# Moving the cosine and spectrum tiles of a three-stage spectral MLP kernel to other start addresses in SBUF

## Chip, cores and metric

One NeuronCore of a Trainium2 chip runs the whole program in one launch. The metric is the device time of that launch in microseconds (us); less is better. The engines are named as in the profile: PE is TensorE's matmuls, PEld its weight loads, DVE is VectorE, ACT ScalarE, POOL GpSimd, and SP the engine that issues most of the DMAs.

## What is computed

The input x has 4 batches of 3136 rows by 256 columns. Three layers follow each other, all in float32:

```python
def _attn_ref(x, filt_r, filt_i):                 # layer 0: a filter along the rows
    X = np.fft.rfft(x, axis=1)
    return np.fft.irfft(X * (filt_r + 1j * filt_i)[None], n=x.shape[1], axis=1)

def _moe_ref(x, w_ch1, w_ch2):                    # layer 1: two-dimensional FFT, then an MLP
    u = x + np.real(np.fft.fft(np.fft.fft(x, axis=1), axis=2))
    un = (u - mean(u)) / np.sqrt(var(u) + 1e-06)
    return u + np.maximum(un @ w_ch1, 0.0) @ w_ch2   # 256 -> 1024 -> 256

def _moe2_ref(x, g_ln, w_ch1, w_ch2):             # layer 2: a second MLP
    xn = (x - mean(x)) / np.sqrt(var(x) + 1e-06) * g_ln
    return x + np.maximum(xn @ w_ch1, 0.0) @ w_ch2
```

## The kernel before

**Spectrum.** The Fourier transforms of 3136 = 64 x 49 points are matrix products with small matrices of sines and cosines. Batch 0 goes first and alone (`first_p` and `first_q`, matmuls on L365, L382, L320, L426 and L454); batches 1 to 3 are done later, in pieces between the work of the MLPs (`over_p` and `over_q`, with the four-quadrant matmuls of `quarter` on L267 and the transposes on L618). Their results are a table `zt` of the filtered spectrum, in SBUF, and the half-transformed rows `vd`, in DRAM.

**Units.** The 12544 rows are handled as 24 units U of 512 rows and a last one of 256. `prep_ticks(U)` makes the input u of layer 1 for a unit: ACT and DVE split a slice of `zt` into a high and a low part (`zs`, tiles `zsh` and `zsl`, for the last unit `zslh` and `zsll`, with the copy `zmid` for one column), and PE multiplies these with a split cosine table (`chi`, `clo`) in 12 matmuls of 128 x 256:

```python
        for a in range(2):
            for eo in (1, 0):
                for i, (s, r) in enumerate(PASSES):      # ("h","h"), ("l","h"), ("h","l")
                    lhs = zmid[...] if eo == 0 and i == 2 else z[a][eo][s]
                    nc.tensor.matmul(out=ps[a][:, eo], lhsT=lhs, rhs=cs[eo][r], ...)     # L731
```

The operand `lhsT` is what PE holds still (a weight load, PEld, brings it), and `rhs` is what it streams past. So `zs` and `zmid` are loaded and `chi` and `clo` stream. Sixteen quarter matmuls of the rows `vr` (L267, 64 x 64 x 256) follow and end the unit's u.

**MLPs.** For each unit and layer the rows are normalised, turned (by transposes on PE, L831, or by a DVE transpose and a trip through DRAM) and split into `xth` and `xtl`. Then `w1_step` streams them against loaded weights `w1a` or `w1b` (L904), ACT and DVE evict the hidden rows into `hh` and `hl`, and `w2_step` loads these and streams `w2a` or `w2b` (L931). All operands of L731, L904 and L931 are 4-byte fp32r; each matmul has its own weight load, and each streams 256 columns.

**Order.** The order on every engine is written out by hand: eight hidden blocks of (U, layer) in turn, with the ticks of `prep_ticks`, `ln_ticks`, `over_p` and `over_q` hung on numbered steps. `prep_ticks` always puts its 12 matmuls behind a `w1_step` of the MLP and before the 16 quarter matmuls.

**Addresses.** SBUF tiles are laid out pool after pool, in the order in which the pools are opened. `gap(name, words)` opens a pool that holds one unused tile of so many 4-byte words, which pushes everything behind it. `PAD` is the list of the gaps' sizes.

Of the kernel before, what the change touches and what calls it, by code (L numbers as in the profile page):

```python
# [158 lines left out]
    return c.astype(np.float32)  # L159


PAD = (24, 16, 48, 48, 16, 32, 16)
NA, LAG = 3, 3
AHEAD = 3
DURING = {4: 'a', 8: 'a', 12: 'a', 16: 'a', 18: 'k', 20: 'a', 24: 'ac', 26: 'a', 28: 's', 30: 'f', 31: 'c', 33: 'f', 34: 'c', 35: 'f', 37: 'f', 38: 'c'}
# [18 lines left out]
def spectral_mlp_kernel(ctx: ExitStack, tc, x, ff, ff0, cst, w1a, w2a, gln, w1b, w2b, out):  # L184
# [4 lines left out]
    def pool(name, bufs, **kw):  # L189
        return ctx.enter_context(tc.tile_pool(name=name, bufs=bufs, **kw))  # L190

    def gap(name, words):
        pool(name, 1).tile([128, words], F32, name=name)

    sm = pool("sm", 4)
    head = pool("head", 1)
    gap("gap0", PAD[0])
    keep = pool("keep", 1)
    gap("gap1", PAD[1])
    keep64 = pool("keep64", 1)  # L200
    uop = pool("uop", 1)
    gap("gap2", PAD[2])
    wp1 = pool("wp1", 1)
    gap("gap3", PAD[3])
    wp2 = pool("wp2", 1)
    wps = {"1": wp1, "2": wp2}
    dram = pool("dram", B, space=DRAM)
    ztp = pool("ztp", 2)
    gap("gap4", PAD[4])
    zsp = pool("zsp", 1)  # L210
    raw = pool("raw", 2)
    vrp = pool("vrp", 2)
# [6 lines left out]
    up = pool("up", 3)  # L219
    xnp = pool("xnp", 1)  # L220
    xdp = pool("xdp", 2, space=DRAM)
    gap("gap5", PAD[5])
    xtp = pool("xtp", 2)
    gap("gap6", PAD[6])
    hp = pool("hp", 2)
    banks = pool("banks", 8, space=PSUM)

# [897 lines left out]
def _launch(inputs):  # L1125
# [58 lines left out]
    with tile.TileContext(nc) as tc:  # L1184
        spectral_mlp_kernel(tc, *args)
# [22 lines left out]
```

## Time and profile before

| | us |
|---|---|
| median of 3 runs | 1345.98 |
| lowest and highest of them | 1345.86, 1347.0 |
| the profiled execution, its own time | 1346.94 |
| its span, first to last instruction | 1345.2 |

PE is busy for 1317.5 us of the span, PEld for 1211.0, DVE for 796.5, ACT for 616.9, POOL for 270.5. Busy time of PE overlaps itself: one matmul takes some 280 ns from start to end, and the next one starts some 113 ns after it. So the pace of PE is read from the distance between starts, and a group of n matmuls in the timeline has n such distances up to the start of the next group. The granted clock of TensorE is at full speed for nearly the whole span (mean 0.992).

### The profile page before, as it was taken

The page shows a single profiled execution, that of the slowest core. Times are in us where ns is not written, and L with a number is a line of the kernel's source. Part 1 is how long each engine was busy: PE and PEld are TensorE (multiplying, and loading weights), DVE is VectorE, ACT ScalarE, POOL GpSimd, SP SyncE. Part 2 cuts the span into 40 slices and gives each one's busy share as a digit, 9 for nine tenths or more (in the row PEclk, how much of TensorE's full clock was granted, in tenths as well). Part 3 has the DMA queues.
Part 4 walks back from the last instruction along what each step waited for, and adds up shares of the span by engine and source line. Part 5 has one row for each costly group of instructions (what it writes and reads, how often), then busy time and mean ns, then how long its engine had stood idle before and what let it go on. Part 6 is the DMA issues. An engine that isn't in the chain of part 4 may idle for free.

```text
span 1345.2 us, 27766 instructions
## 1 busy us (share of the span) xinstructions
PE 1317.5 (98%) x11221; PEld 1211.0 (90%) x11221; DVE 796.5 (59%) x1643; ACT 616.9 (46%) x1205; POOL 270.5 (20%) x277
## 2 busy tenths in 40 slices
PE   8969999999999999999999999999999999999998
PEld 6527998899989989999988999999999999999998
DVE  5968875666454666656454665656555555465453
ACT  5646544454435444544434544545434443444322
POOL 1763012332040222212032221312000000000000
PEclk9979999999999999999999999999999999999999
DMA  8754323443544634623353535534221413332200
GB/s 315 253 192 146 101 92 76 154 115 86 134 140 136 153 91 116 165 62 95 89 170 104 161 106 123 147 81 111 56 64 48 95 34 77 80 83 45 64 17 24
DMA packets 214920, 147.97 MB, mean 110 GB/s; under 512 B 163516, under 2 KB 187196, under 8 KB 214792
## 3 DMA queue, kind: packets, MB, share of 16 engines
q1 hardware_dynamic: 198056, 117.36, 33.6%
q10 hardware_dynamic: 16736, 28.84, 5.9%
q8 instruction: 88, 1.44, 0.5%
q14 instruction: 40, 0.33, 0.1%
HBM read 87.71 MB, written 58.46 MB: 109 GB/s over the span
## 4 chain that ended last, share of the span: by engine, by line
PE 92%; DVE 4%; DMA 1%; ACT 1%; issue 1%; POOL 1%; SPq 0%; ACTq 0%; DVEq 0%; POOLq 0%
PE ps L931 39%; PE ps L904 38%; PE ps L267 7%; PE ps L731 2%; PE ps L320 2%; PE ps L365 1%; PE ps L426 1%; PE ps L618 1%; PE ps L831 1%; PE ps L382 0%; DVE hl L914 0%; DMA vd<-vst 0%; DVE bs L775 0%; DMA gd<-gst 0%; DVE wm L873 0%
## 5 line engine op out<-in xcount | busy, mean ns | idle before, releaser
L914 DVE SCALAR_TENSOR_TENSOR hl<-ps,hh 128x512 fp32r<-128x512 f32 (+1 forms) x400 | 269.5, 675 | 328.6 <-ACT hh L913 323.1
L913 ACT ACTIVATE hh<-ps 128x512 fp32r<-128x512 f32 (+1 forms) x400 | 233.6, 586 | 359.1 <-PE ps L931 314.9
L904 PE MATMUL ps<-xth,w1a 128*128 128x256 f32 x1568 | 243.0, 276 | 0.0
L904 PE MATMUL ps<-xth,w1b 128*128 128x256 f32 x1568 | 242.5, 276 | 0.0
L931 PE MATMUL ps<-w2a,hh 128*128 128x256 f32 x1568 | 219.5, 282 | 0.0
L931 PEld LDWEIGHTS ps<-w2a,hh 128*128 128x128 f32 x1568 | 194.4, 189 | 27.0 <-issue 24.6
L931 PE MATMUL ps<-w2b,hh 128*128 128x256 f32 x1568 | 215.1, 279 | 0.5 <-ACT hh L913 0.5
L904 PEld LDWEIGHTS ps<-xth,w1a 128*128 128x128 f32 x1568 | 207.9, 188 | 1.3 <-issue 1.3
L904 PEld LDWEIGHTS ps<-xth,w1b 128*128 128x128 f32 x1568 | 207.5, 188 | 0.0
L931 PEld LDWEIGHTS ps<-w2b,hh 128*128 128x128 f32 x1568 | 193.2, 188 | 15.4 <-issue 13.8
L779 POOL TENSOR_TENSOR rs<-rs,mhalf 128x4 f32<-128x4 f32 (+1 forms) x51 | 50.9, 997 | 591.6 <-DVE rs L778 506.6
L904 PE MATMUL ps<-xtl,w1a 128*128 128x256 f32 x784 | 154.6, 277 | 0.0
L904 PE MATMUL ps<-xtl,w1b 128*128 128x256 f32 x784 | 154.3, 276 | 0.0
L790 ACT ACTIVATE xn<-u,nb,rs 128x256 f32<-128x256 f32 x152 | 120.3, 840 | 49.5 <-DVE nb L783 47.6
L931 PE MATMUL ps<-w2b,hl 128*128 128x256 f32 x784 | 122.0, 277 | 1.3 <-DVE hl L914 1.3
L931 PE MATMUL ps<-w2a,hl 128*128 128x256 f32 x784 | 121.9, 277 | 1.1 <-DVE hl L914 1.1
L904 PEld LDWEIGHTS ps<-xtl,w1a 128*128 128x128 f32 x784 | 118.7, 188 | 0.6 <-DVE xtl L825 0.6
L904 PEld LDWEIGHTS ps<-xtl,w1b 128*128 128x128 f32 x784 | 118.7, 188 | 0.2 <-DVE xtl L834 0.2
L931 PEld LDWEIGHTS ps<-w2b,hl 128*128 128x128 f32 x784 | 103.8, 188 | 2.1 <-DVE hl L914 2.1
L931 PEld LDWEIGHTS ps<-w2a,hl 128*128 128x128 f32 x784 | 104.2, 188 | 1.3 <-DVE hl L914 1.3
L935 DVE TENSOR_TENSOR u<-ps,u 128x512 f32<-128x512 f32 x98 | 63.1, 685 | 44.4 <-PE ps L931 44.4
L775 DVE BATCH_NORM_STATS2 bs<-u 128x6 f32<-128x256 f32 x196 | 68.6, 411 | 0.0
(146 smaller groups left out, 1449.1 us busy)
## 6 DMA issues: line engine op xcount, KB each, us to landing
xd<-xn SPq DMA_DIRECT2D x38, 512.0 KB
xtl<-xd SPq DMA_DIRECT2D x152, 128.0 KB
fc<-in_ff SPq DMA_DIRECT2D x34, 512.0 KB
vr<-vd SPq DMA_DIRECT2D x48, 256.0 KB
out<-u SPq DMA_DIRECT2D x24, 512.0 KB
vd<-vst ACTq DMA_DIRECT2D x21, 512.0 KB
xr<-in_x SPq DMA_DIRECT2D x18, 512.0 KB
gd<-gst ACTq DMA_DIRECT2D x36, 256.0 KB
```

The lines of the kernel that those rows point to most:

```text
L267: nc.tensor.matmul(out=o[c:c + 64], lhsT=lhs[r:r + k], rhs=rhs[r:r + k], **{"start": True, "stop": True, **kw})
L320: nc.tensor.matmul(out=o, lhsT=cf[at // 512][:k, at % 512:at % 512 + w], rhs=rhs[:k, c0:c1], start=start, stop=stop)
L365: nc.tensor.matmul(out=ps[:, o:o + 128], lhsT=x[:, j, a * 128:a * 128 + 128], rhs=cf[0][:, :128], start=True, stop=True)
L731: nc.tensor.matmul(out=ps[a][:, eo], lhsT=lhs, rhs=cs[eo][r], start=eo == 1 and i == 0, stop=False, skip_group_check=True)
L775: nc.vector.bn_stats(out=st[:, t], in_=u[:, t])
L779: nc.gpsimd.tensor_tensor(out=rs[:, tl], in0=rs[:, tl], in1=mhalf[:, tl], op=ALU.pow)
L790: nc.scalar.activation(out=xs[t], in_=u[:, t].rearrange("p (k a j) -> p j k a", k=2, j=4), func=ACTF.Identity, scale=rs[:, t:t + 1], bias= ...
L904: nc.tensor.matmul(out=ps[:, c:c + 256], lhsT=w[:, a, k, m * 128:m * 128 + 128], rhs=xt[s][:, k, c:c + 256], start=i == 0, stop=i == len(t ...
L913: nc.scalar.activation(out=h[:, :n], in_=ps[:, :n], func=ACTF.Relu)
L914: nc.vector.scalar_tensor_tensor(out=l[:, :n], in0=ps[:, :n], scalar=0.0, in1=f32(h[:, :n]), op0=ALU.max, op1=ALU.subtract)
L931: nc.tensor.matmul(out=o[:, t % 2], lhsT=a[:, t * 128:t * 128 + 128], rhs=w[:, b, m], start=m == 0 and i == 0 and t % 2 == 0, stop=m == 7 ...
L935: nc.vector.tensor_tensor(out=u[:, t - 1:t + 1], in0=o, in1=u[:, t - 1:t + 1], op=ALU.add)
```

## The change

Seven gaps become five, with other sizes; the pools keep their order, and tiles, loops and instructions stay as they are. On every engine the instructions stand in the same order as before. Line numbers behind the first hunk are two lower.

```diff
-PAD = (24, 16, 48, 48, 16, 32, 16)
+PAD = (72, 16, 48, 48, 16)
@@
     sm = pool("sm", 4)
     head = pool("head", 1)
     gap("gap0", PAD[0])
     keep = pool("keep", 1)
     gap("gap1", PAD[1])
     keep64 = pool("keep64", 1)
     uop = pool("uop", 1)
+    wp1 = pool("wp1", 1)
     gap("gap2", PAD[2])
-    wp1 = pool("wp1", 1)
-    gap("gap3", PAD[3])
     wp2 = pool("wp2", 1)
...
     ztp = pool("ztp", 2)
-    gap("gap4", PAD[4])
     zsp = pool("zsp", 1)
...
     xnp = pool("xnp", 1)
-    gap("gap5", PAD[5])
+    gap("gap3", PAD[3])
     xtp = pool("xtp", 2)
-    gap("gap6", PAD[6])
+    gap("gap4", PAD[4])
     hp = pool("hp", 2)
```

Where the tiles start in each partition, modulo 256 bytes, from the allocations of the two built programs:

| tiles | before | changed |
|---|---|---|
| `chi`, `clo` (streamed on L731) | 0 | 192 |
| `zslh`, `zsll`, `zmid`, `uo` | 64 | 0 |
| `zsh`, `zsl`, and `t2` of batch 0 | 64 | 0 |
| `xr`, `xf`, `vr`, `gr`, `fc`, `t`, `y`, `z`, `vst`, `gst`, `u`, `xn`, `f2s` | 64 | 0 |
| `w1a`, `w1b` (loaded on L904); `hh`, `hl` (loaded on L931); `cr` | 0 | 0 |
| `xth`, `xtl` (streamed on L904); `w2a`, `w2b` (streamed on L931) | 192 | 192 |
| `con` (small matrices and the identity, which transposes stream) | 128 | 128 |
| `zt` (two tiles) | 192, 96 | 192, 96 |

A slice of `zs`, `zmid`, `chi`, `clo`, `w1`, `w2`, `xt` or `hh` that a matmul takes starts a multiple of 512 bytes behind its tile's start, so it has the tile's remainder.

## Rows read from the trace of the kernel before

**Rows 1.** The page: busy time by engine, the chain that ended last.

```profile
PE 1317.5 (98%) x11221; PEld 1211.0 (90%) x11221; DVE 796.5 (59%) x1643; ACT 616.9 (46%) x1205; POOL 270.5 (20%) x277
...
PE 92%; DVE 4%; DMA 1%; ACT 1%; issue 1%; POOL 1%; SPq 0%; ACTq 0%; DVEq 0%; POOLq 0%
PE ps L931 39%; PE ps L904 38%; PE ps L267 7%; PE ps L731 2%; PE ps L320 2%; PE ps L365 1%; PE ps L426 1%; PE ps L618 1%; PE ps L831 1%; PE ps L382 0%; DVE hl L914 0%; DMA vd<-vst 0%; DVE bs L775 0%; DMA gd<-gst 0%; DVE wm L873 0%
```

**Rows 2.** Groups of PE, 105 us to the end: line, operation, tiles, count | busy us, mean ns.

```profile
L904 PE MATMUL ps<-xth,w1b 128*128 128x256 f32 x1568 | 242.5, 276 | 0.0
...
L731 PE MATMUL ps<-chi,zsl 128*128 128x256 f32 x92 | 25.9, 281 | 0.0
```

**Rows 3.** Timeline of PE around one unit's cosine products: start us, length us, line, tiles, count.

```profile
783.40 0.39 PE L904 MATMUL ps<-xtl,w1a 128*128 128x256 f32 x2
783.63 0.28 PE L731 MATMUL ps<-chi,zsh 128*128 128x256 f32 x1
...
784.92 0.28 PE L731 MATMUL ps<-clo,zmid 128*128 128x256 f32 x1
785.13 1.09 PE L267 MATMUL ps<-vr,con 64*64 64x256 f32 x16
786.16 0.74 PE L931 MATMUL ps<-w2a,hh 128*128 128x256 f32 x4
```

**Rows 4.** Timeline of PE in MLP steps a few us behind that unit.

```profile
789.00 1.07 PE L931 MATMUL ps<-w2a,hh 128*128 128x256 f32 x8
789.91 0.62 PE L931 MATMUL ps<-w2a,hl 128*128 128x256 f32 x4
790.36 0.39 PE L904 MATMUL ps<-xth,w1b 128*128 128x256 f32 x2
```

**Rows 5.** Timeline of PE in MLP steps of another stretch.

```profile
770.09 1.10 PE L931 MATMUL ps<-w2a,hh 128*128 128x256 f32 x8
771.03 0.64 PE L931 MATMUL ps<-w2a,hl 128*128 128x256 f32 x4
771.50 0.63 PE L904 MATMUL ps<-xth,w1a 128*128 128x256 f32 x4
```

**Rows 6.** PE in seven stretches of MLP steps: stretch us, length, busy (matmuls), granted clock, DMA.

```profile
102.70:112.30 9.60, 9.60 (x83) 1.00 0.77 218
...
764.30:772.75 8.45, 8.45 (x73) 1.00 0.59 195
sum 39.50, PE 39.50; mean PE 5.64
```

**Rows 7.** Timeline of PE where an MLP step hands over to a transpose of `z`.

```profile
287.95 0.40 PE L904 MATMUL ps<-xtl,w1b 128*128 128x256 f32 x2
288.18 0.60 PE L618 MATMUL ps<-con,z 128*128 128x128 f32 x4
```

**Rows 8.** The chain of waits, 0 to 95 us, in order of time: start us, us, what.

```profile
4.05 13.76 PE ps L365 x96
...
26.83 0.44 PE ps L382 x4
...
75.56 3.38 DMA vd<-vst
...
79.58 4.38 DMA gd<-gst
...
84.66 2.50 DMA vd<-vst
...
87.73 3.06 DMA vr<-vd
```

**Rows 9.** PE by stretches of low granted clock, columns as in rows 6.

```profile
81.59:95.24 13.65, 8.42 (x41) 0.50 0.65 195
...
129.37:132.79 3.42, 3.35 (x16) 0.50 0.29 93
```

## Prediction
> **What bounds the kernel now.** I read the page first. PE is busy for 98% of the span and holds 92% of the chain that ended last; 77% of the chain is the two MLP lines L931 and L904, and L731, the cosine products, has 2% [rows 1]. No other engine comes near. So whatever lets PE start its next matmul sooner comes off the end, and whatever happens on DVE, ACT, POOL or the queues counts only where PE waits for it.
>
> A change of addresses alone can act on PE only through the pace, so the groups of PE came next. A matmul of the MLPs takes 276 ns from start to end, one of the cosine products with the same 128 x 256 shape and type takes 281 [rows 2]. Those are lengths; the pace is the distance between starts, and for that I took the timeline. In an MLP stretch 12 matmuls, from 789.00 to 790.36, take 1.36 us: **113.3 ns each** [rows 4]. In the cosine products, from the first start at 783.63 to the twelfth at 784.92, eleven distances take 1.29 us: **117.3 ns each** [rows 3]. The two matmuls of L904 ahead of them start 0.23 us before: 113 and some 117, so the slower pace begins with the distance in which the first `zs` is loaded. Rows 3 are one of 24 such units; the other 23 read alike.
>
> What differs is where the operands lie. In L904 and L931 the loaded operand starts at 0 and the streamed one at 192 (modulo 256 bytes); in L731 the loaded one is at 64, the streamed one at 0. The handover from L904 to a transpose, whose loaded `z` is at 64 too, shows the same: the two last distances take 0.23 us [rows 7], 113 and some 117, though the stream is still `xtl` at 192. So in these rows a load from 64 goes with the slower pace, whatever streams.
>
> **The change, part by part.** No instruction is added, removed or moved; the order on every engine and in each queue stays. What changes is the remainder of the start addresses.
>
> *Cosine products (L731).* Loads go from 64 to 0, streams from 0 to 192: just what the MLP lines have. I take the MLP's pace. A unit has twelve distances that end with such a load: the one ahead of the first product and eleven inside. Each is worth 117.3 - 113.3 = 4.0 ns, so a unit gains 0.048 us. There are 25 units; the first runs at about 87 us, where the granted clock is 0.50 [rows 9] and the stream itself takes twice as long, so I give it nothing. 24 x 0.048 = **1.15 us**. It all lies on the path: PE goes from `w1_step` to L731 to L267 without a gap. The step from the last product to the first quarter matmul (784.92 to 785.13) and the quarter matmuls' 1.03 us up to the next L931 [rows 3] are left as they are. Bounds of this part: nothing, and twice 4 ns, should 0 and 192 be better for these tiles than for the MLPs (no row shows a distance under 113 for 256 columns, so I take the lower value).
>
> *Handovers to transposes.* By the order there are 46 places where L904 is followed by L618 or L831, whose loaded `z` and `xn` go from 64 to 0: 46 x 4 ns = **0.2 us**, if the type of the transpose is not the reason. Bounds 0 and 0.3.
>
> *First matmuls of batch 0 (L365).* Loads `xr` go from 64 to 0, while `cr` streams from 0, a pair that no row shows. The 96 on the chain take 13.76 us, the transposes L382 of the same 128 columns 0.44 us for four [rows 8]; the loaded tile of the latter starts at many remainders and they keep 0.11 us. At 4 ns either way 100 matmuls are +-0.4 us; I take 0.
>
> *Quarter matmuls (L267).* `con` is loaded from 128 as before; the streams `xf`, `gr`, `y` and `vr` go from 64 to 0. Sixteen take 1.03 us in rows 3, 0.26 us for four that run side by side. 1024 matmuls make 256 such groups; at 4 ns a group +-1.0 us. No row shows the new pair; I take 0, since the rows tie the pace to the loaded operand, and that one stays.
>
> *Other engines.* DVE, ACT and POOL read and write at 0 what they had at 64. They are off the path; I take 0. Should a hidden row become slower by a few ns, it is covered by PE, busy without a break in most stretches.
>
> *DMAs.* Loads and stores of the spectrum tiles go from 64 to 0. On the chain four transfers of the head matter: 3.38, 4.38, 2.50 and 3.06 us, together 13.3 us [rows 8]. No row shows the same transfer at another remainder; I take 0, and a tenth of the sum, 1.3 us, as the bound on either side. The Trainium skill (DMA: Bandwidth & Descriptors, How a descriptor splits into AXI transactions) says that a descriptor that begins off a 256-byte boundary fetches from the boundary below; for 2048 bytes from 64 its beats would be 66 and not 64, an estimate of 3%, 0.4 us of these 13.3. No run here shows it.
>
> **Sum.** 1.15 + 0.2 = 1.4 us less. The profiled execution took 1346.94 us (span 1345.2), so 1345.5 us; it stands 0.96 us above the median of the three runs, 1345.98, and against that the forecast is **1344.6 us**. That is 0.1%. About 0.2%, 2.7 us, is what a measurement of this kernel tells from no change.
>
> **Rivals.**
>
> *1. The place has nothing to do with it: no gain.* The slower pace also occurs at the MLPs' own places: 770.09 to 771.50, twelve matmuls of L931 in 1.41 us, 117.5 ns each [rows 5], loaded from 0, streamed from 192. So 117 may be a state of PE's pipeline that L731 enters for another reason, such as its order of operands. Against it: all 24 warm units show the slower pace from the first `zs` load on, coming from 113, while the MLP stretches are fast but for seven. The time would stay at 1346.0. The Trainium skill (SBUF — State Buffer, SBUF: two separate sides) speaks for this rival: it gives PE one read port for the moving operand and one for the weight load, independent of each other, and lets PE's ports wait for nobody. By that rule no remainder could matter and the sum would be zero; that all 24 units keep 117 ns where the MLP next to them has 113 speaks against it, as far as the traces go. Chance 0.20, with the case that the tiles don't land where they should (the allocations of the built program say that they do).
>
> *2. More than the cosine products gets faster.* Seven stretches of MLP steps, 39.5 us together [rows 6], run at the slower pace of rows 5. Each begins behind a break in PE's stream (quarter matmuls, a transpose or a wait) and lasts until the next one. If the other placement makes PE leave those breaks in the fast state, 39.5 x (117.5 - 113.3) / 117.5 = 1.4 us more go, 1343.2 in all. Apart from that, the granted clock falls to 0.50 in three stretches, the shortest of 3.4 us [rows 9], each after a wait of PE; work of 3.4 us at half clock costs 1.7 us over full clock. If a DMA in the head comes in sooner and one such stretch is not granted, that is 1.7 us: 1341.5 with both. Chance 0.15 that the whole is over 2.7 us.
>
> *3. Slower: more MLP stretches fall into the slow pace.* The same mechanism backwards. By the order PE comes back to the MLP lines 116 times (70 times from L267, 46 from L618 or L831), with some 80 matmuls each time. A stretch of 80 at 4.2 ns more costs 0.34 us; today seven are slow. The breaks' last loads and streams are what moves, so their phase may too. It decides the sign once more than four further stretches are slow, and goes over 2.7 us with twelve: 12 x 0.34 - 1.4 = 2.7, so 1348.7; with all 46 transposes' returns slow it would be 1360. For it: rows 5 show that a stretch at 0 and 192 can lock at 117. Against it: 109 of 116 returns end fast with `z` and `xn` loaded from 64 and from `con` alike, so the break seems to matter more than the place. Chance 0.05.
>
> **How the numbers follow.** My forecast 0.60 (a gain between 0.7 and 2.2 us), rival 1 0.20, rival 2 0.15, rival 3 0.05. The first two are within 0.2%: same 0.80, faster 0.15, slower 0.05. The range begins where rival 2 has one of its two gains and the bounds of DMA and quarter matmuls add to it, 1344.6 - 1.4 - 1.0 = 1342.2, and ends where rival 1 meets the loss of one more clock step's half or of three more slow stretches, 1346.0 + 1.0 = 1347.0. Ten in a hundred are left out below, and some eight above.
>
> **What would show it.** Right: in the timeline the eleven distances of a unit's cosine products take 1.25 us, not 1.29, and the mean length of L731 falls from 281 to 276 ns; the quarter matmuls behind keep 1.03 us. Handovers to L618 go from 0.23 to 0.226 us for two. Rival 1: L731 keeps 281. Rival 2 and 3: L731 is as forecast, but MLP stretches at 117 ns add up to clearly less or more than 39.5 us, or the stretches at clock 0.50 become fewer or longer. Wrong altogether: a new wait of PE, or quarter matmuls whose sixteen take over 1.1 us.

## The result

The changed kernel takes 1363.83 us (median of 4 runs, 1362.89 to 1366.17) where the kernel before takes 1345.92 (4 runs, 1345.31 to 1347.0): a ratio of **1.0135**, 95% interval 1.0119 to 1.0151. It is 1.3% slower; the prediction said 1344.6, between 1342.2 and 1347.0. The profiled execution took 1363.67 us, with a span of 1361.9, which is 16.7 us more than before.

The page of the changed kernel looks much as in [rows 1]: PE 98% busy, nearly the same shares of the chain, and the other engines with the same busy time to within 0.6 us. Only PE and its weight loads have more of it:

```profile
PE 1333.5 (98%) x11221; PEld 1229.0 (90%) x11221; DVE 796.8 (59%) x1643; ACT 616.6 (45%) x1205; POOL 269.9 (20%) x277
...
PE ps L929 39%; PE ps L902 38%; PE ps L265 7%; PE ps L729 2%; PE ps L318 1%; PE ps L363 1%; PE ps L616 1%; DVE xtl L823 1%; PE ps L829 1%; PE ps L424 1%; DVE hl L912 0%; DMA ww<-in_w2a 0%; DMA fc<-in_ff 0%; PE ps L380 0%; DMA gd<-gst 0%
```

The groups of PE from 105 us to the end (line, operation, tiles, count | busy us, mean ns) show where: the cosine products got shorter, 279 ns where [rows 2] have 281, and the MLP matmuls, whose addresses did not change, longer, 279 where they had 276:

```profile
L902 PE MATMUL ps<-xth,w1b 128*128 128x256 f32 x1568 | 246.1, 279 | 0.0
...
L729 PE MATMUL ps<-chi,zsl 128*128 128x256 f32 x92 | 25.6, 279 | 0.0
```

A mean of 279 is a mixture. PE by stretches of 40 us late in the program, changed kernel (stretch us, length, busy (matmuls), granted clock, DMA):

```profile
1050.00:1090.00 40.00, 40.00 (x342) 1.00 0.35 80
1100.00:1140.00 40.00, 40.00 (x355) 1.00 0.36 80
1145.00:1185.00 40.00, 40.00 (x342) 1.00 0.35 80
...
1240.00:1280.00 40.00, 40.00 (x342) 1.00 0.32 80
```

and the kernel before in the same part of the program:

```profile
1085.00:1125.00 40.00, 40.00 (x355) 1.00 0.35 80
1130.00:1170.00 40.00, 40.00 (x355) 1.00 0.35 80
```

Some two matmuls of each count overlap the edges, so 355 is a matmul every 113.4 ns and 342 one every 117.8: the two paces of [rows 4] and [rows 5]. Before, all these stretches are fast; now every second one is slow. The clock is granted in full in all of them, and the DMA engines are as busy in the fast as in the slow. From here on a *break* is a place where PE does something else between two MLP stretches (transposes, quarter matmuls, cosine products), a *return* is its way back, and a return is called slow when the distances between starts behind the first five are 116 to 119 ns, fast when they are 113 or 114. Of the 9292 distances between MLP matmuls, 466 were slow before and 4905 are now; 4439 x 4.3 ns is **19.1 us**. Against that stand 1.4 us by which the first MLP matmul starts earlier (101.04 us, before 102.45) and 1.6 us less in the breaks. The sum is 16.1 of the 16.7 us; the rest is MLP distances outside the two bands (all 9292 together grew by 19.8 us).

The breaks tell which returns went over. Timeline of the changed kernel behind four transposes of `z` (start us, us, line, tiles, count), the place that [rows 7] show before:

```profile
287.75 0.60 PE L616 MATMUL ps<-con,z 128*128 128x128 f32 x4
288.11 1.19 PE L929 MATMUL ps<-w2b,hh 128*128 128x256 f32 x8
289.13 0.64 PE L929 MATMUL ps<-w2b,hl 128*128 128x256 f32 x4
289.60 0.64 PE L902 MATMUL ps<-xth,w1b 128*128 128x256 f32 x4
290.07 0.40 PE L902 MATMUL ps<-xtl,w1b 128*128 128x256 f32 x2
290.31 0.40 PE L902 MATMUL ps<-xth,w1b 128*128 128x256 f32 x2
```

From 289.13 ten distances take 1.18 us: slow. Before, the same ten, from 289.54 to 290.67, took 1.13:

```profile
289.54 0.62 PE L931 MATMUL ps<-w2b,hl 128*128 128x256 f32 x4
289.99 0.62 PE L904 MATMUL ps<-xth,w1b 128*128 128x256 f32 x4
290.45 0.39 PE L904 MATMUL ps<-xtl,w1b 128*128 128x256 f32 x2
290.67 0.50 PE L904 MATMUL ps<-xth,w1b 128*128 128x256 f32 x3
```

And, in the changed kernel, around a unit's cosine products:

```profile
423.58 0.39 PE L902 MATMUL ps<-xtl,w1a 128*128 128x256 f32 x2
423.81 0.28 PE L729 MATMUL ps<-chi,zsh 128*128 128x256 f32 x1
...
425.05 0.28 PE L729 MATMUL ps<-clo,zmid 128*128 128x256 f32 x1
425.26 1.09 PE L265 MATMUL ps<-vr,con 64*64 64x256 f32 x16
426.28 1.21 PE L929 MATMUL ps<-w2a,hh 128*128 128x256 f32 x8
427.33 0.63 PE L929 MATMUL ps<-w2a,hl 128*128 128x256 f32 x4
427.80 0.64 PE L902 MATMUL ps<-xth,w1a 128*128 128x256 f32 x4
428.27 0.40 PE L902 MATMUL ps<-xtl,w1a 128*128 128x256 f32 x2
```

The eleven distances of the cosine products (423.81 to 425.05) now take 1.24 us, some 113 ns each (113.4 by the starts before rounding), as forecast; in [rows 3] they took 1.29. But behind them the MLP comes back slow: 427.33 to 428.27, eight distances, 0.94 us. The 0.05 us gained inside is paid back at once: on average 155 matmuls follow up to the next break, and 4.3 ns more on each are 0.67 us.

Over the whole trace: 25 of 27 returns from L616 (`z`) are slow where none was; and of the 22 units whose break goes straight back to the MLP, ten entered the cosine products fast and came back slow, twelve entered slow and came back fast. So with the loads at 0 these breaks turned the pace over, 48 of 49 times. With 64, all 22 cosine breaks and all 27 transposes of `z` came back fast; but all of them were entered fast too. What keeps the slow share near half is mostly the breaks of quarter matmuls alone: of the 23 that were entered slow 20 came back fast.

### The profile page after: what moved, and what is told of

Its sections match the earlier page's. It is cut to its first block, busy times and chain, and to the rows that moved or that the text cites. A ratio compares the mean times of both kernels' runs of the same rounds, so it can differ in the third digit from the quotient of the medians.

```text
span 1361.9 us, 27766 instructions
## 1 busy us (share of the span) xinstructions
PE 1333.5 (98%) x11221; PEld 1229.0 (90%) x11221; DVE 796.8 (59%) x1643; ACT 616.6 (45%) x1205; POOL 269.9 (20%) x277
## 4 chain that ended last, share of the span: by engine, by line
PE 91%; DVE 4%; DMA 2%; ACT 1%; issue 1%; POOL 1%; ACTq 0%; SPq 0%; POOLq 0%; DVEq 0%
PE ps L929 39%; PE ps L902 38%; PE ps L265 7%; PE ps L729 2%; PE ps L318 1%; PE ps L363 1%; PE ps L616 1%; DVE xtl L823 1%; PE ps L829 1%; PE ps L424 1%; DVE hl L912 0%; DMA ww<-in_w2a 0%; DMA fc<-in_ff 0%; PE ps L380 0%; DMA gd<-gst 0%
## 5 line engine op out<-in xcount | busy, mean ns | idle before, releaser
L902 PE MATMUL ps<-xth,w1a 128*128 128x256 f32 x1568 | 246.4, 279 | 0.0
L902 PE MATMUL ps<-xth,w1b 128*128 128x256 f32 x1568 | 246.1, 279 | 0.0
L929 PE MATMUL ps<-w2a,hh 128*128 128x256 f32 x1568 | 222.6, 284 | 0.0
L929 PE MATMUL ps<-w2b,hh 128*128 128x256 f32 x1568 | 218.7, 282 | 0.4 <-ACT hh L911 0.4
L902 PEld LDWEIGHTS ps<-xth,w1b 128*128 128x128 f32 x1568 | 210.4, 188 | 0.0
L929 PEld LDWEIGHTS ps<-w2b,hh 128*128 128x128 f32 x1568 | 196.2, 188 | 15.4 <-issue 13.8
```

The lines of the kernel that those rows point to most:

```text
L902: nc.tensor.matmul(out=ps[:, c:c + 256], lhsT=w[:, a, k, m * 128:m * 128 + 128], rhs=xt[s][:, k, c:c + 256], start=i == 0, stop=i == len(t ...
L929: nc.tensor.matmul(out=o[:, t % 2], lhsT=a[:, t * 128:t * 128 + 128], rhs=w[:, b, m], start=m == 0 and i == 0 and t % 2 == 0, stop=m == 7 ...
```

## The experiments

Each ran beside the kernel before on one chip, but not all on the same one, so medians of different groups of rows are best compared by their ratios. What they gave, in one table; "L618" and "L731" are the lines of the kernel before. "Slow" counts are returns behind breaks that contain that line, and MLP distances of 116 to 119 ns among the 9292, all read from the starts in the one profiled execution of each kernel.

| run | loads `zs` / `z` from | slow returns L618 (27) | slow returns L731 (24) | slow MLP distances | median us | ratio (95% interval) |
|---|---|---|---|---|---|---|
| before | 64 / 64 | 0 | 0 | 466 | 1345.9 | |
| changed | 0 / 0 | 25 | 10 | 4905 | 1363.8 | 1.0135 (1.0119 to 1.0151) |
| e1_cos | 64 / 64 | 0 | 1 | 506 | 1346.4 | 0.9998 (0.9988 to 1.0007) |
| e2_z | 64 / 0 | 24 | 9 | 3736 | 1359.7 | 1.0095 (1.0080 to 1.0110) |
| e3_zs | 0 / 64 | 2 | 17 | 3862 | 1360.3 | 1.0101 (1.0086 to 1.0116) |
| e4_z64 | 64 / 64 | 0 | 1 | 829 | 1348.6 | 1.0014 (1.0004 to 1.0023) |
| e5_s128z192 | 128 / 192 | 1 | 22 | 4304 | 1361.4 | 1.0107 (1.0066 to 1.0147) |
| e6_s192z128 | 192 / 128 | 0 | 0 | 407 | 1346.2 | 1.0000 (0.9989 to 1.0012) |
| e7_s32z96 | 32 / 96 | 21 | 23 | 7164 | 1376.9 | 1.0221 (1.0186 to 1.0257) |
| e8_s96z32 | 96 / 32 | 23 | 22 | 7016 | 1376.0 | 1.0215 (1.0178 to 1.0252) |
| e9_more1 | 64 / 0 | 0 | 0 | 457 | 1349.3 | 1.0031 (1.0018 to 1.0045) |
| e9_more3 | 64 / 0 | 0 | 0 | 290 | 1353.9 | 1.0053 (1.0030 to 1.0076) |
| e11_con | 0 / 64 | 2 | 16 | 3874 | 1361.2 | 1.0106 (1.0055 to 1.0156) |
| e12_quarters1 | 0 / 64 | 0 | 1 | 565 | 1354.4 | 1.0062 (1.0038 to 1.0087) |
| e12_quarters2 | 0 / 64 | 0 | 1 | 656 | 1359.9 | 1.0103 (1.0082 to 1.0124) |
| e14_first | 0 / 64 | 2 | 19 | 3920 | 1364.3 | 1.0136 (1.0119 to 1.0153) |

### Which of the moved tiles does it

Four kernels take the change apart; only gaps differ.

**e1_cos:** `chi` and `clo` alone.

```diff
-PAD = (24, 16, 48, 48, 16, 32, 16)
+PAD = (72, 32, 48, 48, 16, 32, 16)
```

> Edit: of the change, only chi and clo move (0 to 192); all spectrum tiles stay at 64. Theory T1 (the tile that is LOADED in a break of PE's stream sets the pace at which the MLP matmuls come back: loaded from 64 they come back fast; loaded from 0 a fast stretch comes back slow and a slow one fast): zs is still loaded from 64, so the cosine products stay slow (length 281 ns), the returns stay fast, 1346 us, within 1.5. Rival T2 (what is STREAMED sets it): the cosine products fall to 276 ns, and some or all of the 24 returns behind them come back slow, 1353 to 1362 us. Rival T3 (any shift deals the paces out anew, without a rule): somewhere between 1344 and 1385 us, with slow returns behind breaks of any kind.

Measured: no change in the time. The cosine products on `chi` stay at 282 and 281 ns, and the returns stay fast. The streams' place is not quite without effect: the distances inside the cosine products go from 117.5 to 118.1 ns, which over 24 units is under 0.2 us. T2 falls.

**e2_z:** `z` alone.

```diff
+    gap("gapz", 48)
     zp2 = pool("zp2", 3)
+    gap("gapy", 16)
```

> Edit: the kernel before with z alone at 0 (64 before). T1: the 27 returns from the transposes of z come back slow, the 24 behind the cosine products fast; about 2690 MLP matmuls at 4.3 ns more are 10 to 12 us, so 1356 to 1358 us. T2: z is never streamed, so nothing changes, 1346 us. T3: slow returns of any kind.

Measured: 24 of 27 returns from `z` slow (the other three were entered slow and came back fast), 13 us. That is 1.7 us more than T1 said, since a slow stretch that enters the cosine products (loads at 64) also came back slow in nine units, which T1 had left out.

**e3_zs:** `zs` and `zmid` at 0, `chi` and `clo` at 192.

```diff
-PAD = (24, 16, 48, 48, 16, 32, 16)
+PAD = (72, 16, 0, 48, 0, 32, 16)
...
-    gap("gap2", PAD[2])
...
-    gap("gap4", PAD[4])
     zsp = pool("zsp", 1)
+    gap("gap4", 16)
```

> Edit: chi and clo at 192, and zs, zsl, zmid and uo at 0, as in the change; z, xn, vr and the other spectrum tiles stay at 64. T1: all cosine products of the 24 warm units run at 113 ns (1.2 us less), all 24 returns behind them come back slow, about 3680 MLP matmuls at 4.3 ns, 16 us; the returns from z fast. 1359 to 1362 us. T2 (the stream vr at 0 makes the return slow): cosine products fast and returns fast, 1344.8 us. T3: slow returns of any kind.

Measured: within T1's range, though T1 had all 24 units fast inside and slow behind, and it was 17. All 17 units of the straight kind that entered fast came back slow, all 5 that entered slow came back fast; inside, these kept 117.7 ns although `zs` was loaded from 0.

**e4_z64:** the changed kernel with `zs`, `zmid` and `z` put back to 64.

```diff
-PAD = (72, 16, 48, 48, 16)
+PAD = (72, 32, 48, 48, 16)
...
     uop = pool("uop", 1)
+    gap("gapw", 48)
...
+    gap("gaps", 16)
     zsp = pool("zsp", 1)
+    gap("gapt", 48)
...
+    gap("gapz", 16)
     zp2 = pool("zp2", 3)
+    gap("gapy", 48)
```

> Edit: the changed kernel with zs, zsl, zmid, uo and z back at 64; chi and clo stay at 192, and xr, gr, y, vr, xn, u and the other spectrum tiles at 0. T1: cosine products slow, returns from them and from z fast; only the 19 returns from the transposes of xn may be slow (at most 4 us, some 1 us), and the head keeps the 1.4 us that the changed kernel gained before the first MLP matmul: 1344 to 1347 us. T2: the streams are as in the changed kernel, so 1360 us and more. T3: anything between 1344 and 1385 us.

Measured: 1348.6 us, 1.6 above that range. Six returns from transposes of `xn` (still at 0) are slow, and slow distances cost some 1.6 us more than before. Whether the 1.4 us of the head belong to the change is not shown: over the traces of the kernels here the first MLP matmul starts between 101.0 and 104.8 us, without a pattern. Putting back these three sets of tiles leaves 0.14% of the 1.35%: the loads of `z` and `zs` are the cause; the streams and the rest make up that 0.14% (interval 0.04 to 0.23).

### Is 0 bad and 64 good?

The next four put `zs` and `z` at other places (gaps as in e2_z and e3_zs, other sizes).

> Edit: the kernel before with chi and clo at 192, zs, zsl, zmid and uo at 128, z at 192; the rest at 64. Which start addresses are like 0 and which like 64? Ta (only the remainder modulo 128 counts: 128 is like 0, 192 like 64): cosine products at 113 ns and their returns slow, returns from z fast, 1360 us as with zs alone at 0. Tb (64 alone brings fast returns): returns behind both slow where a fast stretch enters, 1360 to 1366 us. Tc (0 alone brings slow ones): both fast, 1344 to 1347 us.

> Edit: as the one before, with zs, zsl, zmid and uo at 192 and z at 128. Ta: cosine products slow, their returns fast, returns from z slow, 1357 to 1360 us as with z alone at 0. Tb: both slow, 1360 to 1366 us. Tc: both fast, 1344 to 1347 us.

> Edit: as before, with zs, zsl, zmid and uo at 32 and z at 96. Half-way places: Tb: both returns slow, 1360 to 1366 us. Tc: both fast, 1344 to 1347 us. Ta says nothing of odd multiples of 32; if a start at 32 costs a load the same as one at 64 (the load then straddles as many lines), both are fast too, 1344 to 1347 us.

> Edit: as before, with zs, zsl, zmid and uo at 96 and z at 32. Tb: both returns slow, 1360 to 1366 us. Tc: both fast, 1344 to 1347 us. As for 32 and 96 themselves: this one and the one before put each of the two in each of the two breaks, so a difference that goes with the place, and not with the tile, shows as the two swapped.

None of the three rules holds. Behind `z`, 128 and 192 come back fast, 32 and 96 nearly always keep the pace with which they were entered (21 of 21 slow entries came back slow in each run, 10 of 12 fast ones fast). Behind `zs`, 192 comes back fast, and 128, 32 and 96 slow. The same 128 is good for one break and bad for the other. With 32 and 96 these breaks hardly turn a slow stretch back any more (1 of 36 slow entries in the first of the two runs, 1 of 38 in the second), and three quarters of the MLP distances are slow: some 30 us. So no rule in the remainder holds for both breaks. (The gaps move the higher part of an address too; it was not varied by itself.)

### The place or the moment

A hint lies in the fine timing. In all runs so far, where PE enters the cosine products fast, the first distance behind the 16 quarter matmuls is 220 to 223 ns before a fast stretch and 225 or 226 before a slow one. (For slow entries it tells less: in e2_z nine slow stretches follow 221 or 222.) The next runs change no address and shift the return.

**e9_more1 and e9_more3:** e2_z with one, or three, transposes done again.

```diff
             Z = bank().rearrange("p (t a k) -> p t a k", t=2, a=2)
+            for _ in range(1):          # 3 in e9_more3
+                nc.tensor.transpose(Z[:, 0, 0], z[:, 0, 0], ident)
```

> Edit: the kernel with z alone at 0, and in each of the 27 transpose breaks the first transpose is done once more (same result, no address changed). It costs 27 times 0.109, 2.9 us. Two readings of why z at 0 makes returns slow. Tp (timing: where in PE's fine rhythm the first MLP load behind the break comes; the address acts through the few ns that it adds in the break): one transpose more shifts the return, and so some or most of the 27 returns become fast; with all fast the time is 1346.7 + 2.9, about 1350 us. Ta (the place of the last load itself decides): returns stay slow, 1359.7 + 2.9, about 1362.6 us.

> Edit: as the one before, with the first transpose done three times more, 8.8 us. Tp: the shift is another one; returns fast or slow in another share than with none or one more, 1355 to 1368 us (all fast 1355.5, all slow 1368.5). Ta: slow, 1368.5 us.

Here Ta no longer is the rule modulo 128 but the rival of timing. Timeline of e2_z, `z` loaded from 0:

```profile
288.33 0.60 PE L620 MATMUL ps<-con,z 128*128 128x128 f32 x4
288.69 1.19 PE L933 MATMUL ps<-w2b,hh 128*128 128x256 f32 x8
289.71 0.63 PE L933 MATMUL ps<-w2b,hl 128*128 128x256 f32 x4
290.18 0.63 PE L906 MATMUL ps<-xth,w1b 128*128 128x256 f32 x4
290.65 0.40 PE L906 MATMUL ps<-xtl,w1b 128*128 128x256 f32 x2
290.89 0.64 PE L906 MATMUL ps<-xth,w1b 128*128 128x256 f32 x4
```

and of e9_more1, the same addresses and one transpose more:

```profile
287.04 0.27 PE L619 MATMUL ps<-con,z 128*128 128x128 f32 x1
287.15 0.60 PE L622 MATMUL ps<-con,z 128*128 128x128 f32 x4
287.50 1.17 PE L935 MATMUL ps<-w2b,hh 128*128 128x256 f32 x8
288.51 0.62 PE L935 MATMUL ps<-w2b,hl 128*128 128x256 f32 x4
288.96 0.62 PE L908 MATMUL ps<-xth,w1b 128*128 128x256 f32 x4
289.42 0.39 PE L908 MATMUL ps<-xtl,w1b 128*128 128x256 f32 x2
289.64 0.62 PE L908 MATMUL ps<-xth,w1b 128*128 128x256 f32 x4
```

Ten distances from 289.71 take 1.18 us in the first, ten from 288.51 take 1.13 in the second. All 27 returns are fast with one more and with three more. **More work is faster**: 1349.3 us against 1359.7, some 9 us by the two ratios. Ta falls, and Tp's forecast came. Strictly, a transpose more shifts the return and also adds a load, and these two runs do not part the one from the other.

**e11_con:** e3_zs with `con` at 192.

```diff
-PAD = (72, 16, 0, 48, 0, 32, 16)
+PAD = (56, 16, 0, 48, 0, 32, 16)
...
+    gap("gaph", 16)
     head = pool("head", 1)
```

> Edit: the kernel with zs at 0 and chi at 192 (cosine products fast, 1360 us), with con, from which the quarter matmuls behind them load and which transposes stream, at 192 and not 128. Tp: the quarter matmuls' loads come otherwise, so the first distance behind them moves from 226 ns, and the 24 returns may become fast; with all breaks fast 1345 us, a little below the kernel before. Ta (the place of the loads of zs decides): 226 ns and slow as before, 1360 us. Either way the transposes, which now stream from 192, may return otherwise.

Measured: nothing moved (225 or 226 ns as before, 16 slow returns), so where `con` is loaded from doesn't shift the return. By itself that fits both readings.

**e12_quarters1 and e12_quarters2:** e3_zs with two, or four, quarter products added again.

```diff
         for eo in (1, 0):
-            for a in range(2):
+            for a in (0, 1, 1) if eo else (0, 1):     # (0, 0, 1, 1) in e12_quarters2
                 for h in range(2):
                     quarter(ps[a][:, eo], 64 * (h ^ a), const("i2"), ...)
```

> Edit: the kernel with zs at 0 and chi at 192 (cosine products fast, returns behind them slow, 1360.3 us), and in every such break the last two quarter products are added once more, which is one group of four passes, some 0.215 us, 5.4 us in all; no address is changed. It leaves a wrong sum in u. Tp (timing): the return is shifted by a fraction of PE's rhythm and may become fast: all fast 1360.3 - 16 + 5.4 = about 1350 us. Ta (the loads of zs from 0 decide): returns slow, first distance 226 ns, 1365.7 us.

> Edit: as the one before, with two groups more (four quarter products added once more), 10.8 us; u is wrong again. Tp: another shift, all fast 1355 us, all slow 1371 us, and between this run and the one before at least one should be fast. Ta: both slow, this one 1371 us.

Timeline of e12_quarters1 at the unit shown for the changed kernel:

```profile
424.68 0.28 PE L730 MATMUL ps<-clo,zmid 128*128 128x256 f32 x1
424.89 1.53 PE L266 MATMUL ps<-vr,con 64*64 64x256 f32 x20
426.35 1.19 PE L930 MATMUL ps<-w2a,hh 128*128 128x256 f32 x8
427.37 0.62 PE L930 MATMUL ps<-w2a,hl 128*128 128x256 f32 x4
427.82 0.62 PE L903 MATMUL ps<-xth,w1a 128*128 128x256 f32 x4
428.28 0.39 PE L903 MATMUL ps<-xtl,w1a 128*128 128x256 f32 x2
428.50 0.62 PE L903 MATMUL ps<-xth,w1a 128*128 128x256 f32 x4
```

From 427.37 ten distances take 1.13 us. The returns of all units but one are fast in both runs, and the cosine products of 22 and 23 units run at 113.4 ns, with `zs` loaded from 0. The times lie 4 to 5 us above the "all fast" of the expectations. In e12_quarters1 that is the passes: four more cost 0.44 us a unit (1.46 for twenty, 1.02 for sixteen), twice the 0.215 assumed. In e12_quarters2 the break is hardly longer than that. Its trace is 6.7 us longer than that of e12_quarters1, of which 2.0 lie ahead of the first MLP matmul, 3.3 in breaks without cosine products and 1.3 in waits inside MLP stretches; why is open. It is not in slow MLP distances. The counts decide, and they speak against Ta for this break too.

**e14_first:** e3_zs with the quarter matmuls ahead of the cosine products.

```diff
+        for eo in (1, 0):
...
+            quarter(ps[a][:, eo], ..., start=eo == 1, stop=False, ...)
         for a in range(2):
             for eo in (1, 0):
                 for i, (s, r) in enumerate(PASSES):
-                    nc.tensor.matmul(..., start=eo == 1 and i == 0, stop=False, ...)
+                    nc.tensor.matmul(..., start=False, stop=eo == 0 and i == 2, ...)
...
-        for eo in (1, 0):
...
-            quarter(ps[a][:, eo], ..., start=False, stop=eo == 0, ...)
```

> Edit: the kernel with zs at 0 and chi at 192, with the quarter matmuls put ahead of the cosine products (the first ones open the sums, the last cosine products close them). The result is the same. The break then ends with matmuls of the MLPs' own shape, so PE's rhythm is set once, where the cosine products begin, and goes on into the MLP. Tp: all 24 units are fast through and through, or slow through and through, as that one phase comes out: 1344 to 1345.5 us if fast (a little below the kernel before), 1360 us and more if slow. Ta: cosine products and MLP fast, 1344 to 1345.5 us.

Timeline of one unit:

```profile
427.40 1.09 PE L266 MATMUL ps<-vr,con 64*64 64x256 f32 x16
428.43 0.39 PE L735 MATMUL ps<-chi,zsh 128*128 128x256 f32 x1
428.65 0.28 PE L735 MATMUL ps<-chi,zsl 128*128 128x256 f32 x1
...
429.82 0.28 PE L735 MATMUL ps<-clo,zmid 128*128 128x256 f32 x1
429.94 1.10 PE L930 MATMUL ps<-w2a,hh 128*128 128x256 f32 x8
430.88 0.64 PE L930 MATMUL ps<-w2a,hl 128*128 128x256 f32 x4
```

From 428.65 to 429.82 ten distances take 1.17 us, and on to 430.88 nine more 1.06: slow through and through, in 19 of 24 units; the other five are fast through and through. So the pace is dealt once, where the first matmuls of that shape follow the quarter matmuls, and goes on from the cosine products into the MLP. Here it is dealt badly, 1364 us. Tp said that all units would come out alike; they did not: of the 20 that entered the break fast 19 became slow, and the four that entered slow became fast. The first distance behind the quarter matmuls is 225 or 226 ns in the 19 and 221 to 224 in the five.

## Why the prediction was wrong

**What held.** The tiles landed where they should, no other engine, queue or wait took part, and the cosine products did go to 113 ns wherever PE entered them fast (121 of 264 distances); the others ran at 117.7 from the same place. The breaks together became 1.6 us shorter. That this is near the 1.4 of the sum is chance: 0.6 us lie in the breaks with cosine products, where the sum had 1.15, 0.2 at the transposes, as the sum had it, and 0.9 in the breaks of quarter matmuls alone, where it had nothing. The first unit, left out for its granted clock of 0.50, has 213 ns for most distances in both kernels (not quite the "twice as long"), so it gained nothing, as said.

**The step that failed** is the one that treated the pace as local to the moved loads: "I take the MLP's pace" for the cosine products, while the steps behind them "are left as they are", and with them the pace of the MLP behind every break. In the sum the MLP's own matmuls stand with no term at all. The runs showed that the pace of the 9292 MLP distances is set at each return, and that the loads of `z` and `zs` in the breaks change it: 4439 distances more went slow, 19.1 us. One return decides over the 80 matmuls that follow on average, 0.34 us, seven times the 0.048 us that a unit's cosine products could gain.

**Rival 3** named that mechanism and its price, and said that twelve further slow stretches make 1348.7. It got 0.05, because "109 of 116 returns end fast with `z` and `xn` loaded from 64 and from `con` alike". That was read as robustness. The runs speak for the opposite, that a placement in which nearly all returns are fast is a tuned state and most shifts leave it: of seven placements of `zs` and `z` tried besides the one before, only 192 / 128 is as good; the changed kernel, e2_z, e3_zs, e5, e7 and e8 are 1.0 to 2.2% slower. The range should have reached at least to all 46 transposes slow, which the text itself priced at 1360.

**Rival 1** is half right in a way that was not foreseen: the place as such has no steady price for the MLP, and rows 5 did show a state of PE. The Trainium skill (SBUF — State Buffer, SBUF: two separate sides) gives the moving operand and the weight load independent read ports, by which no placement could change PE's time; e2_z, in which one loaded tile starts at 0 and not at 64 (modulo 256 bytes) and the kernel takes 1.0% longer, speaks against drawing that from it. The measurement decides. Whether the two ports meet somewhere is not shown by these runs.

**Not settled:** why a load from another place shifts the return by a few ns, and what in PE makes two paces of the same instructions stable. The runs show that the pace lasts until the next break or the next wait of PE: in all 16 traces no stretch changes its pace lastingly without a distance of over 140 ns. They show that the return selects it, by more than the place of the loads. That it is the moment of the return is the reading that fits best (e9, e12, and the 220 to 223 against 225 or 226 ns behind fast entries); the nine slow stretches of e2_z behind 221 or 222 ns show that this distance alone doesn't decide, and the unit of that rhythm was not measured.

**Is there a version that beats both?** An estimate from the distances: all MLP returns fast and the cosine products at 113 ns would give 1.2 us over the kernel before, and its remaining slow distances 2.0 more at most. e12_quarters1 has nearly that state and pays 10 us for it in extra passes. A free shift of the same kind was not tried beyond e14_first, which came out slow.

## What to carry to other kernels

When PE is the bound and its matmuls follow each other without a gap, read the distance between starts in each stretch, and look whether it has two values. If it has, an edit between the stretches, one of addresses as well as one of instructions, can deal them out anew, and its price is (matmuls behind each break) x (difference of the paces), not the cost of the edit. Judge such an edit by the count of slow stretches in the trace, and take an attained good state as fragile when giving a range.

## What was not expected of the hardware

- The same MLP instructions at the same addresses run at 113.3 or 117.7 ns for hundreds of matmuls on end (up to 454 in the changed kernel), at full granted clock; the choice is made at the return from a break or a wait.
- With `z` at 0, adding a transpose of 0.109 us to each of 27 breaks made the kernel some 9 us faster (1.0095 to 1.0031 of the kernel before; medians 1359.7 and 1349.3 us).
- Where two loaded tiles start modulo 256 bytes moved the whole program by 0 to some 30 us (ratios 1.0000 to 1.0221), with no rule in the remainder that held for both breaks.
- Where a streamed tile starts (`chi`, `clo` at 0 or 192) made no difference to the time that could be measured: 0.9998, 0.9988 to 1.0007.
